# Words of w1 fetched a pair ahead, a product bank taken from attention's pool, and batch 1's attention one border sooner

## The chip, the cores and the metric

The kernel runs on one core of one Trainium2 chip. The metric is the device time of one execution in microseconds (us). One profiled execution is shown as a trace; all rows quoted here are from it. The engines are called PE (matrix multiplications; PEld is its loading of weights), DVE (vector engine), ACT (scalar engine), POOL (GpSimd) and SP (which here only issues transfers). SBUF is the on-chip memory, PSUM the eight banks that PE writes its sums into.

## The reference

Two layers follow each other. The first is attention in chunks of 32 tokens, each with a context of 16 tokens to its left and 8 to its right and 8 memory tokens (4 batches, 8 heads, 768 tokens, 64 channels a head). The second mixes tokens with a product of rank 32 and channels with a two-layer network:

```python
scores = scale * np.matmul(q_c, k_full.transpose(0, 1, 3, 2))
a = np.exp(scores - max); a = a / (sum(a) + 1e-9)
out[:, :, c_start:c_end] = np.matmul(a, v_full)
...
h = x.transpose(0, 2, 1) @ U @ V
u = x + h.transpose(0, 2, 1)
ch = np.maximum(u @ w_ch1, 0.0) @ w_ch2          # 512 -> 2048 -> 512
return u + ch
```

U, V and both weights arrive as 64-bit floats. The kernel decodes them on the chip into a float32 value, which it splits into a high and a low half for PE.

## The kernel before, in words

Each of the 4 batches has 768 tokens, in two blocks of 384. Hidden channels come in 16 groups f of 128.

**Batch 0** (`both_blocks`) goes through 32 units n. Units 0 to 17 take groups 0 to 8 of both blocks in turn, 18 to 24 groups 9 to 15 of block 0, 25 to 31 groups 9 to 15 of block 1. A unit is a w1_step (12 matmuls of 384 columns, L1178) and then a w2_step (9 matmuls of 512 columns, L1231 and L1236), which belongs to the unit before it. Unit 24 does two w2_steps, so unit 25 has none. Meanwhile the weights are decoded: ACT and DVE use the V buffers `vbs` (vb_104, vb_105, vbe) as working space, and the decoded values of each w1 group are kept in DRAM (`val_d`, vald in the rows).

**Batches 1 to 3** (`fast`, `seven`) replace the first layer of the network, for the two blocks and a pair p of groups at once, by seven products instead of eight (a Strassen scheme). Pairs p run from 0 to 7. `products(p)` does seven products of 6 matmuls each, in three PSUM banks b1, b2, b3, in the order b1, b2, b3, b1, b2, b3, b1. After each, ACT or DVE reads the bank: L1448 and L1454 (ACT, b1), L1450 and L1457 (DVE, b2), L1452 and L1459 (DVE, b3), L1461 (DVE, b1 after the last). The banks are drawn from two pools: ps_h (2 banks) and ps_a (3 banks, shared with attention and its turnings). Which bank of a pool one gets is the one that comes free first.

The seven weight factors of pair p+1 are made ahead, during products(p): `prepare` fetches the values of both groups (POOL's queue, L1335) into two rotating slots called val and lets POOL form five sums (L1341); `build_factor` casts a sum, or a half of the fetched words, on ACT (L1410) and takes the rest on DVE (L1411). ACT, DVE and POOL each work their instructions off in the order written, and POOL issues its transfers in that same order.

After products(p), `first_block` runs the second layer for block 0 (two w2_steps), except after products(0) and products(4), where the next products follow at once. After pair 3 and after pair 7 `second_block` runs block 1's second layer, its three accumulators being two ps_h banks and one ps_a bank.

**Attention of batch b+1** is woven into batch b at borders. It is a generator whose steps are, for each pair of heads s = 0 to 3: scores(s) (L713, then the softmax on DVE and ACT), the turning of its weights (L745, six transposes), and the weighing of V (L756). Then come the gathering of the token product (L864, L1057), two groups of three matmuls that add it to x (L1081, with the additions L1083), and the fold (L1363 to L1378), which turns x into the operands th and tl of the products. In batch 0 the list PLAN says at which of 26 borders (two in each of the units 19 to 31, one before the w1_step and one after it) a step is taken. From unit 29 on, `following` runs what is left of the attention and one third of the fold after the border.

The third in order is SP's queue: it issues the loads of q, k and v for the attention (L508, L527, L531) in the order in which the generator asks for them, between stores and loads of the low halves of w1 (L356, L437).

Of the kernel before, what the change touches and what calls it, by code (L numbers as in the profile page):

```python
# [9 lines left out]
F32 = mybir.dt.float32  # L10
# [36 lines left out]
RATEL = 6  # L47
RATES = 8
RATEB = 5
PLAN = [0, 1, 0, 0, 0, 1, 1, 1, 0, 1, 1, 1, 0, 1, 1, 1, 0, 1, 1, 1, 1, 1, 0, 0, 0, 0]  # L50
SUMS = ((0, 0, 0, 0, 1, "add"), (2, 0, 0, 1, 1, "add"), (4, 1, 0, 1, 1, "add"),
        (5, 0, 1, 1, 1, "subtract"), (6, 1, 0, 0, 0, "subtract"))
PRODUCTS = ((6, 0), (2, 1), (0, 2), (1, 0), (5, 1), (4, 2), (3, 0))
# [4 lines left out]
def chunk_attn_then_mixer_kernel(  # L58
# [13 lines left out]
    nc = tc.nc  # L72
# [1172 lines left out]
    def both_blocks(following):  # L1245

        units = []
        for f in range(SPLIT + LEAD):
            if f < SPLIT:
                units.append((0, f, 0, f == 0, None))  # L1250
            if f >= LEAD:
                g = f - LEAD
                units.append((1, g, 1, g == 0, False if g == SPLIT - 1 else None))
        units += [(0, f, 0, False, True if f == NF - 1 else None) for f in range(SPLIT, NF)]
        units += [(1, f, 0, f == SPLIT, True if f == NF - 1 else None) for f in range(SPLIT, NF)]
        prev = []
        for n, (blk, f, where, begins, ends) in enumerate(units):
            while done[0] < min(2 * NF, 2 * f + 1 + (n > LATE)):
                advance(1)
                more_w()  # L1260
            if n == 2:
                head.close()
            let_go()
            solo = n >= 2 * SPLIT
            if n == 2 * SPLIT:
                paced.close()
            for blk_, m, *_ in units[n:n + AHEAD + 1]:
                if m >= SPLIT and blk_ == 1:
                    get_w1l(m)
            w1l = w1ls[f]  # L1270
            if f >= SPLIT or blk == 1:
                del w1ls[f]
            if n == 2 * SPLIT - SOON or 2 * SPLIT - LAID <= n < 2 * SPLIT - LAID + 2:
                place(1)
            serve(RATEL if n < 2 * SPLIT else RATES)
            if n > 2 * SPLIT:
                border()
            if n == 0:
                for c, g3 in rest[:2]:
                    join_uT1(turn_x1(c), c, g3)  # L1280
            if n == len(units) - 1:
                for m in range(3):
                    build_factor(0, m)
            hid_ = w1_step(0, blk, f, w1l)
            if n == len(units) - 2:
                prepare(0)
            if n == len(units) - 5:
                open_turned()
            if n == len(units) - 1:
                open_fast()  # L1290
                for m in range(3, len(PRODUCTS)):
                    build_factor(0, m)
            if n == 0:
                decode(2, 4)
                for c, g3 in rest[2:]:
                    join_uT1(turn_x1(c), c, g3)
                decode(1, 1)
                decode(2, 6)
                decode(1, 6)
                decode(3, 2)  # L1300
            for _ in range(RATE + (3 < n < 12)):
                advance(1)
                more_w()
            if n > 2 * SPLIT:
                border()
            if n >= len(units) - 3:
                following()
            prev.append((blk, f, where, begins, ends) + hid_)
            if solo or n % 2 == 0 or ends:
                while len(prev) > (not ends):  # L1310
                    while done[0] < 2 * prev[0][1] + 2:
                        advance(1)
                        more_w()
                    w2_step(0, *prev.pop(0))
# [12 lines left out]
    def border():  # L1327
        place(PLAN[at[0]])
        at[0] += 1

    def prepare(p):

        whole = [slot([P, NCK, P], F32, "val") for _ in range(2)]
        for side in range(2):
            nc.gpsimd.dma_start(out=whole[side], in_=val_d[2 * p + side])  # L1335
        mixed[p, 1], mixed[p, 3] = whole[1][:, 2:4, :], whole[0][:, 0:2, :]
        for m, (n, fa, ca, fb, cb, op) in enumerate(SUMS):
            if m % 2 == 0:
                two = slot([P, 2, 2, P], F32, "sums")
            a, b_ = (whole[f][:, 2 * c:2 * c + 2, :] for f, c in ((fa, ca), (fb, cb)))  # L1340
            nc.gpsimd.tensor_tensor(out=two[:, m % 2], in0=a, in1=b_, op=getattr(ALU, op))  # L1341
            mixed[p, n] = two[:, m % 2]
# [80 lines left out]
    def seven(b, kept, last):  # L1423

        th, tl = turned[0]
        ta, tb = fast_pools[1]
        made = {}

        def products(p):
            banks = [ps_h.tile([P, 512], F32, name="ps_h"), ps_a.tile([P, 512], F32, name="ps_a")]  # L1430
            banks.append(ps_h.tile([P, 512], F32, name="ps_h"))
            banks = [bank_[:, :TOK] for bank_ in banks]
            b1, b2, b3 = banks
            kept[2 * p], kept[2 * p + 1] = (
                fast_pools[0].tile([P, TOK], F32, name="kept", bufs=NF // 2) for _ in range(2)
            )
            hid_ = {}
            for n, (i, at_) in enumerate(PRODUCTS):
                s = factors.pop((p, n))
                parts = [(s, c, t, c) for c in range(2) for t in (th, tl)] + [(s, 2 + c, th, c) for c in range(2)]  # L1440
                for m, (w, wc, t, c) in enumerate(parts):
                    nc.tensor.matmul(  # L1442
                        out=banks[at_], lhsT=w[:, wc, :], rhs=t[:, i, c, :], start=(n < 3 and m == 0),
                        stop=(m + 1 == len(parts)), skip_group_check=True,
                    )
                with tc.high_priority(offset=HIGH):
                    if n == 0:
                        nc.scalar.copy(out=ta, in_=b1)  # L1448
                    elif n == 1:
                        nc.vector.tensor_tensor(out=ta, in0=b2, in1=ta, op=ALU.subtract)  # L1450
                    elif n == 2:
                        nc.vector.tensor_tensor(out=tb, in0=b3, in1=ta, op=ALU.add)  # L1452
                    elif n == 3:
                        nc.scalar.copy(out=kept[2 * p], in_=b1)  # L1454
                    elif n == 4:
                        hid_[1] = split_hidden(b2)
                        nc.vector.tensor_tensor(out=tb, in0=tb, in1=b2, op=ALU.subtract)  # L1457
                    elif n == 5:
                        nc.vector.tensor_tensor(out=ta, in0=b3, in1=ta, op=ALU.add)  # L1459
                    else:  # L1460
                        nc.vector.tensor_tensor(out=kept[2 * p + 1], in0=b1, in1=tb, op=ALU.add)  # L1461
                        hid_[0] = split_hidden(ta)
                    if p + 1 < NF // 2 or not last:
                        for m in ((), (), (0,), (1, 2), (), (3, 4), (5, 6))[n]:
                            build_factor((p + 1) % (NF // 2), m)
                if n in (2, 6):
                    fast_border()
            made[p] = hid_

        def first_block(p):  # L1470
            hid_ = made.pop(p)
            for side in (1, 0):
                f = 2 * p + side
                ends = True if p == NF // 2 - 1 and side == 0 else None
                w2_step(b, 0, f, 0, p == 0 and side == 1, ends, *hid_[side])
                fast_border()

        def second_block(fs, ends, each):
            for f in fs:
                hid_ = split_hidden(kept.pop(f))  # L1480
                w2_step(b, 1, f, 2, f == fs[0], ends if f == fs[-1] else None, *hid_)
                each()

        return products, first_block, second_block

    def fast(b, following):
        n = NF // 2
        products, first_block, second_block = seven(b, {}, b == B - 1)
        passed[0] = 0
        for p in range(n):  # L1490
            if p + 1 < n or b + 1 < B:
                prepare((p + 1) % n)
            products(p)
            if p % (n // 2):
                first_block(p - 1)
            if p == n // 2 - 1:
                first_block(p)
                recall(b, 1)
                second_block(list(range(n)), False, fast_border)
        recall(b, 0)  # L1500
        first_block(n - 1)
        recall(b, 1)
        second_block(list(range(n, NF)), True, following)
# [73 lines left out]
```

## Time and profile before

| | |
|---|---|
| median of 3 runs | 653.23 us (651.63 to 653.72) |
| the profiled execution's own time | 654.93 us |
| its span, first to last instruction | 653.2 us |
| PE busy | 619.0 us (95%) |
| DVE, ACT, POOL busy | 458.8, 293.4, 189.9 us |
| mean granted clock of PE | 0.987 of full speed |

PE is busy in 95% of the span, so the time is its work plus its idle stretches. Most of the idle stands in the first 60 us, which the change does not touch. The rest is some twenty waits of 0.2 to 2.1 us. Two stretches of 20 us later on show a granted clock of 0.91. The rows below show each wait with what ended it; a busy share over the whole span would not.

### The profile page before, as it was taken

How to read it: one execution, taken by the hardware profiler on the slowest of the kernel's cores; microseconds unless marked ns; L12 is line 12 of the kernel's file. 1: busy time of each engine (PE TensorE's matmuls, PEld its weight loads, DVE VectorE, ACT ScalarE, POOL GpSimd, SP SyncE). 2: the span in 40 equal slices, each digit the busy share in tenths (PEclk: the TensorE clock that was granted, in tenths of full speed). 3: DMA queues.
4: the chain of work that ended last, by engine and by line, in shares of the span. 5: the costliest groups of instructions: out<-in, count | busy, mean ns of one | idle time of the engine just before them, and what ended most of it. 6: DMA issues, size and time to landing. Idle time of an engine off the chain costs nothing.

```text
span 653.2 us, 15318 instructions
## 1 busy us (share of the span) xinstructions
PE 619.0 (95%) x6052; PEld 537.6 (82%) x6054; DVE 458.8 (70%) x983; ACT 293.4 (45%) x700; POOL 189.9 (29%) x294
## 2 busy tenths in 40 slices
PE   7687999999899999999999999999999999999997
PEld 6556999987786798878898898988798799889986
DVE  4875998889555988756676969766776966427542
ACT  4656776655223545533334545532333643314321
POOL 3520011000002764004631663003731564006400
PEclk9889999999898999999999999999999999999999
DMA  9996679655996239976211439942221442003411
GB/s 204 170 287 253 223 213 247 160 148 140 155 206 126 80 131 167 150 107 130 97 50 65 153 122 153 165 57 82 72 75 43 143 154 82 2 16 97 129 48 50
DMA packets 157082, 84.17 MB, mean 129 GB/s; under 512 B 128978, under 2 KB 143314, under 8 KB 157010
## 3 DMA queue, kind: packets, MB, share of 16 engines
q1 hardware_dynamic: 146034, 47.40, 36.2%
q0 software_dynamic: 10976, 35.79, 16.4%
q8 instruction: 48, 0.79, 0.5%
q14 instruction: 24, 0.20, 0.1%
HBM read 63.63 MB, written 19.40 MB: 127 GB/s over the span
## 4 chain that ended last, share of the span: by engine, by line
PE 59%; issue 18%; DVE 11%; DMA 6%; ACT 2%; POOL 2%; SPq 1%; POOLq 0%; DVEq 0%; ACTq 0%
PE ps_h L1442 17%; PE acc L1231 10%; PE ps_a L1442 7%; PE ps_h L1231 5%; PE acc L1236 5%; PE ps_h L1236 2%; PE ps_a L1231 2%; DVE tl L1378 2%; DMA vb<-in_v_dram 2%; DVE fold L1373 1%; PE ps_a L756 1%; PE ps_a L713 1%; PE ps_a L1236 1%; DMA val<-vald 1%; POOL vald L374 1%
## 5 line engine op out<-in xcount | busy, mean ns | idle before, releaser
L1341 POOL TENSOR_TENSOR sums<-val 128x256 f32<-128x256 f32 x120 | 98.0, 847 | 56.9 <-DMA val<-vald 43.9
L1231 PE MATMUL acc<-w,hh 128*128 128x512 f32 x366 | 98.0, 403 | 1.0 <-DVE w L382 1.0
L1442 PE MATMUL ps_h<-th,w1l 128*128 128x384 f32 x288 | 84.2, 344 | 6.5 <-DVE part L1459 5.0
L1231 PEld LDWEIGHTS acc<-w,hh 128*128 128x128 f32 x366 | 67.9, 190 | 16.2 <-issue 1.8
L1442 PEld LDWEIGHTS ps_h<-th,w1l 128*128 128x128 f32 x288 | 53.0, 188 | 12.1 <-ACT pT L747 3.6
L1418 DVE SCALAR_TENSOR_TENSOR hl<-kept,hh 128x384 fp32r<-128x384 f32 x48 | 28.8, 599 | 40.3 <-PE ps_a L1236 23.0
L1442 PE MATMUL ps_h<-th,s 128*128 128x384 f32 x192 | 52.8, 336 | 0.0
L1236 PE MATMUL acc<-w,hl 128*128 128x512 f32 x183 | 51.9, 392 | 0.0
L1442 PE MATMUL ps_h<-tl,w1l 128*128 128x384 f32 x144 | 49.0, 340 | 0.9 <-DVE tl L1378 0.9
L1417 ACT ACTIVATE hh<-kept 128x384 fp32r<-128x384 f32 x48 | 25.2, 526 | 54.0 <-PE ps_a L1231 29.2
L1231 PE MATMUL ps_h<-w,hh 128*128 128x512 f32 x156 | 43.4, 400 | 0.0
L1178 PE MATMUL ps_h<-uh,w1h 128*128 128x384 f32 x124 | 42.5, 349 | 0.8 <-ACT uh L1150 0.8
L1178 PE MATMUL ps_h<-ul,w1h 128*128 128x384 f32 x124 | 41.2, 340 | 0.0
L1236 PEld LDWEIGHTS acc<-w,hl 128*128 128x128 f32 x183 | 34.4, 189 | 7.8 <-issue 0.2
L1448 ACT COPY part<-ps_h 128x384 f32<-128x384 f32 x24 | 11.5, 480 | 62.8 <-PE ps_h L1442 54.6
L1231 PE MATMUL ps_a<-w,hh 128*128 128x512 f32 x132 | 37.9, 390 | 1.8 <-ACT hh L1184 1.8
L1163 POOL DMA_DIRECT2D xd<-x x9 | 4.9, 543 | 114.5 <-DVE x L1192 113.7
L1410 ACT CAST s<-sums 128x256 fp32r<-128x256 f32 x72 | 28.6, 402 | 17.1 <-PE ps_h L1442 13.7
L1411 DVE TENSOR_TENSOR w1l<-sums,w1l 128x256 fp32r<-128x256 f32 x48 | 25.4, 529 | 14.8 <-ACT w1l L1410 14.8
L1442 PEld LDWEIGHTS ps_h<-th,s 128*128 128x128 f32 x192 | 35.0, 188 | 0.0
L1231 PEld LDWEIGHTS ps_h<-w,hh 128*128 128x128 f32 x156 | 28.2, 188 | 5.7
L1184 ACT ACTIVATE hh<-ps_h 128x384 fp32r<-128x384 f32 x31 | 15.0, 487 | 38.7 <-PE ps_h L1178 38.7
(290 smaller groups left out, 1469.4 us busy)
## 6 DMA issues: line engine op xcount, KB each, us to landing
val<-vald POOLq DMA_DIRECT2D x48, 256.0 KB, 3.1
vb<-in_v_dram SPq DMA_DIRECT2D x23, 336.0 KB
rw<-in_moe_w_ch_dram SPq DMA_DIRECT2D x14, 512.0 KB
x<-xd POOLq DMA_DIRECT2D x27, 256.0 KB, 4.0
raw<-in_moe_w_ch_dram SPq DMA_DIRECT2D x20, 256.0 KB
kall<-in_k_dram SPq DMA_DIRECT2D x48, 96.0 KB
kall<-in_q_dram SPq DMA_DIRECT2D x48, 96.0 KB
out_dram<-x POOLq DMA_DIRECT2D x18, 256.0 KB, 3.0
```

The source lines that it names most:

```text
L1178: nc.tensor.matmul(out=ph[:, :TOK], lhsT=w[:, c, :], rhs=u[c], start=(m == 0), stop=(m + 1 == len(parts)),)
L1184: nc.scalar.activation(out=hh, in_=ph[:, :TOK], func=AF.Relu)
L1231: nc.tensor.matmul(out=acc[tt], lhsT=h[:, sl], rhs=w, start=(begins and m == 0), stop=False,)
L1236: nc.tensor.matmul(out=acc[tt], lhsT=hl[:, sl], rhs=w2h[f], start=False, stop=ends is not None)
L1341: nc.gpsimd.tensor_tensor(out=two[:, m % 2], in0=a, in1=b_, op=getattr(ALU, op))
L1378: nc.vector.tensor_tensor(out=tl[:, i:i + m, :, sl], in0=f32[n][:, 0:m], in1=th[:, i:i + m, :, sl].bitcast(F32), op=ALU.subtract,)
L1410: nc.scalar.copy(out=s[:, 0:2], in_=total)
L1411: nc.vector.tensor_tensor(out=s[:, 2:4], in0=total, in1=s[:, 0:2].bitcast(F32), op=ALU.subtract)
L1417: nc.scalar.activation(out=hh, in_=src, func=AF.Relu)
L1418: vpace[0] = nc.vector.scalar_tensor_tensor(out=hl, in0=src, scalar=0.0, in1=hh.bitcast(F32), op0=ALU.max, op1=ALU.subtract,)
L1442: nc.tensor.matmul(out=banks[at_], lhsT=w[:, wc, :], rhs=t[:, i, c, :], start=(n < 3 and m == 0), stop=(m + 1 == len(parts)), skip_group_c ...
L1448: nc.scalar.copy(out=ta, in_=b1)
```

## The change

Four edits go together.

1. The words of pair p no longer go into rotating slots. They have one fixed place, the last 512 columns of vb_104 and vb_105, which no V of batches 1 to 3 uses. `fetch_words` is taken out of `prepare` and called a pair sooner: for pair p+2 behind products(p).
2. The first sums (`prepare(0)`) move from unit 30 to unit 26; the words of pair 1 are fetched behind unit 31's factors.
3. In products(0) and products(4), b1 is a ps_a bank and b2 a ps_h bank.
4. PLAN loses one of the three zeros in front of its third placement and has one more placement at its end: every step from the first turning on comes one border sooner, and the first three of the additions of the token product come at a border of their own.

```diff
-PLAN = [0, 1, 0, 0, 0, 1, 1, 1, 0, 1, 1, 1, 0, 1, 1, 1, 0, 1, 1, 1, 1, 1, 0, 0, 0, 0]
+PLAN = [0, 1, 0, 0, 1, 1, 1, 0, 1, 1, 1, 0, 1, 1, 1, 0, 1, 1, 1, 1, 1, 1, 0, 0, 0, 0]
...
-            if n == len(units) - 2:
+            if n == len(units) - 6:
+                fetch_words(0)
                 prepare(0)
...
                 for m in range(3, len(PRODUCTS)):
                     build_factor(0, m)
+                fetch_words(1)
...
-    def prepare(p):
+    whole = [
+        vb.rearrange("p i d -> p (i d)")[:, NX * D:NX * D + CH].rearrange("p (c f) -> p c f", c=NCK) for vb in vbs[:2]
+    ]
-        whole = [slot([P, NCK, P], F32, "val") for _ in range(2)]
+    def fetch_words(p):
         for side in range(2):
             nc.gpsimd.dma_start(out=whole[side], in_=val_d[2 * p + side])
+
+    def prepare(p):
+
         mixed[p, 1], mixed[p, 3] = whole[1][:, 2:4, :], whole[0][:, 0:2, :]
...
             banks = [ps_h.tile([P, 512], F32, name="ps_h"), ps_a.tile([P, 512], F32, name="ps_a")]
+            if p % (NF // 4) == 0:
+                banks.reverse()
             banks.append(ps_h.tile([P, 512], F32, name="ps_h"))
...
             products(p)
+            if p + 2 < n or b + 1 < B:
+                fetch_words((p + 2) % n)
```

On PE, in units 21 and 22 of batch 0, the first turning (L745) and the steps behind it move against the w1_step (L1178) and the w2_step (L1231, L1236); L756 is the weighing of heads pair 0, L713 the scores of heads pair 1.

```order
 L1236 MATMUL acc_1273<-w_1788,hl 128x512
 L1236 MATMUL acc_1274<-w_1788,hl 128x512
+L745 MATMUL ps_a<-ident,pt 128x128 x6
 L1178 MATMUL ps_h<-uh,w1h_1912 128x384
 L1178 MATMUL ps_h<-ul,w1h_1912 128x384
...
 L1178 MATMUL ps_h<-uh,w1l 128x384 x4
-L745 MATMUL ps_a<-ident,pt 128x128 x6
+L756 MATMUL ps_a<-vb_104,pT 32x64 x48
 L1231 MATMUL acc_1272<-w_1883,hh 128x512 x2
 L1231 MATMUL acc_1273<-w_1883,hh 128x512 x2
```

The turning now stands ahead of unit 21's w1_step, and the weighing has the turning's old place behind it.

On SP, at the same place, the loads of V for heads pair 1 (L527, L531) stand against two stores and a load of low halves (L356, L437).

```order
 L356 DMA w1ld_126<-w1l 128x512
 L508 DMA kall<-in_k_dram 32x24x32 x4
-L356 DMA w1ld_127<-w1l 128x512
-L356 DMA w1ld_128<-w1l 128x512
-L437 DMA w1l<-w1ld_123 128x512
 L527 DMA vb_104<-in_mem_v_dram 8x24x64
 L531 DMA vb_104<-in_v_dram 56x24x64
 L527 DMA vb_104<-in_mem_v_dram 8x24x64
 L531 DMA vb_104<-in_v_dram 56x24x64
+L356 DMA w1ld_127<-w1l 128x512
+L356 DMA w1ld_128<-w1l 128x512
+L437 DMA w1l<-w1ld_123 128x512
```

The V loads follow the k loads directly, and the three transfers of w1 come behind them.

On POOL, at pair 4 of batch 1, the recall of three x tiles (L1168) and three stores (L1163) stand ahead of the sums of pair 5. Before:

```order
L1168 DMA x<-xd_5_151 128x512
L1163 DMA xd_3_149<-x 128x512
L1163 DMA xd_4_150<-x 128x512
L1163 DMA xd_5_151<-x 128x512
L1335 DMA val<-vald_140 128x512
L1335 DMA val<-vald_141 128x512
L1341 TENSOR_TENSOR sums<-val 128x256 x5
```

And now:

```order
L1339 DMA vb_104<-vald_140 128x512
L1339 DMA vb_105<-vald_141 128x512
L1168 DMA x<-xd_3_149 128x512
L1168 DMA x<-xd_4_150 128x512
L1168 DMA x<-xd_5_151 128x512
L1163 DMA xd_3_149<-x 128x512
L1163 DMA xd_4_150<-x 128x512
L1163 DMA xd_5_151<-x 128x512
L1348 TENSOR_TENSOR sums<-vb_104 128x256
L1348 TENSOR_TENSOR sums<-vb_104,vb_105 128x256
```

The fetch of the words (L1339) has moved ahead of the recall and the stores; the sums (L1348) follow the stores with no fetch between.

## Rows read from the trace of the kernel before

**Rows 1.** Waits of PE, whole span: engine, line, releaser: total us, times, longest.

```profile
PE ps_h L1442 <- DVE part L1459: 5.0, 5, 1.7
PE ps_a L756 <- DMA vb<-in_v_dram: 4.2, 3, 2.1
...
PE ps_h L1442 <- DVE x L1192: 1.0, 2, 0.5
...
PE ps_h L1442 <- DVE tl L1378: 0.9, 2, 0.5
...
PE ps_a L1442 <- DVE tl L1378: 0.7, 1, 0.7
```

**Rows 2.** Timeline of PE, batch 1, pair 5: start us, us, instruction [idle before].

```profile
310.34 0.41 PE L1442 MATMUL ps_h<-th,w1l 128*128 128x384 f32 x1 [1.72 <-DVE part L1459]
310.59 0.34 PE L1442 MATMUL ps_h<-tl,w1l 128*128 128x384 f32 x1
310.77 0.34 PE L1442 MATMUL ps_h<-th,w1l 128*128 128x384 f32 x1
```

**Rows 3.** Timelines of POOL and DVE, batch 1, pair 4.

```profile
305.57 3.87 POOL L1341 TENSOR_TENSOR sums<-val 128x256 f32<-128x256 f32 x5 [3.39 <-DMA val<-vald]
...
308.56 0.54 DVE L1457 TENSOR_TENSOR part<-part,ps_a 128x384 f32<-128x384 f32 x1
...
309.65 0.54 DVE L1459 TENSOR_TENSOR part<-ps_h,part 128x384 f32<-128x384 f32 x1
```

**Rows 4.** Timelines of PE and ACT, batch 0, the first turning.

```profile
146.93 0.96 PE L745 MATMUL ps_a<-ident,pt 128*128 128x128 f32 x6 [1.04 <-ACT pt L734]
...
146.35 0.94 ACT L734 ACTIVATE pt<-pt 128x384 f32<-128x384 f32 x2
```

**Rows 5.** Timelines of PE and DVE, the scores of heads pair 1.

```profile
154.98 1.16 PE L713 MATMUL ps_a<-kall 64*32 64x64 f32 x94 [0.92 <-DVE xa L765]
...
154.38 1.01 DVE L765 TENSOR_TENSOR xa<-ps_a,rs 128x384 f32<-128x384 f32 x2
```

**Rows 6.** Timelines of SP and PE, the load of V for heads pair 1 and its weighing.

```profile
152.25 2.33 SPq L508 DMA_DIRECT2D kall<-in_k_dram  x4
...
161.22 0.48 SPq L531 DMA_DIRECT2D vb<-in_v_dram  x1
...
166.45 1.59 PE L756 MATMUL ps_a<-vb,pT 64*32 64x64 f32 x94 [2.13 <-DMA vb<-in_v_dram]
```

**Rows 7.** Two stretches: busy us of each engine (instructions), granted clock, DMA share, GB/s.

```profile
160.00:180.00 20.00, 16.69 (x260) 14.13 (x259) 12.34 (x31) 6.41 (x16) 1.62 (x3) 0.91 1.00 158
...
200.00:220.00 20.00, 18.93 (x92) 15.49 (x91) 16.33 (x31) 9.27 (x22) 8.77 (x13) 0.91 0.45 107
```

**Rows 8.** Timelines of PE and DVE, the weighing of heads pair 2 and what follows.

```profile
181.22 1.15 PE L756 MATMUL ps_a<-vb,pT 64*32 64x64 f32 x94 [1.30 <-DMA vb<-in_v_dram]
...
179.23 0.56 DVE L1185 SCALAR_TENSOR_TENSOR hl<-ps_h,hh 128x384 fp32r<-128x384 f32 x1 [0.99 <-ACT hh L1184]
...
180.60 0.94 DVE L703 STREAM_TRANSPOSE kall<-kall 128x768 f32<-128x768 f32 x1
```

**Rows 9.** Timeline of PE, the additions and the first fold.

```profile
203.29 0.87 PE L1081 MATMUL ps_a<-g,v 96*128 96x512 f32 x3
...
206.73 1.71 PE L1363 MATMUL ps_a<-ident,xa 128*128 128x128 f32 x8
```

**Rows 10.** Timelines of DVE, POOL and PE, the fold and batch 1's first products.

```profile
210.22 3.31 DVE L1378 TENSOR_TENSOR tl<-fold,th 128x512 fp32r<-128x512 f32 x4
...
217.75 2.21 DVE L1378 TENSOR_TENSOR tl<-fold,th 128x512 fp32r<-128x512 f32 x4
...
211.08 4.80 POOL L1341 TENSOR_TENSOR sums<-val 128x256 f32<-128x256 f32 x5 [2.12 <-DMA val<-vald]
...
228.22 0.44 PE L1442 MATMUL ps_h<-tl,w1l 128*128 128x384 f32 x1 [0.47 <-DVE tl L1378]
```

**Rows 11.** Timeline of POOL, batch 1, pair 0: the sums of pair 2.

```profile
233.76 4.20 POOL L1341 TENSOR_TENSOR sums<-val 128x256 f32<-128x256 f32 x5 [3.08 <-DMA val<-vald]
```

## The prediction

> **What bounds the kernel now.** I read the list of PE's waits first, then the timeline around each, then the two stretches with a lower clock. PE is busy in 95% of the span, so nothing but idle on PE, or its clock, can be won. In the list, four sums belong to places that the change touches: 5.0 us in five waits for L1459, 1.0 in two for the additions L1192, 4.2 in three for V and 1.6 (0.9 and 0.7) in three for tl [rows 1]. The reader is to see that these are small sums of a few waits each, so the change is worth single microseconds a place. In the timelines the reader is to look at who was late: for L1459 it is the sums on POOL, two engines back [rows 3].
>
> What a wait costs beyond its idle: matmuls last 0.34 us but start 0.18 apart (310.59, 310.77), and the first after a wait is followed after 0.25 [rows 2]. The pipe has to fill again, 0.16 and 0.07 us; I count 0.25 a wait.
>
> **Part A: banks and words in batches 1 to 3.** The first bank of products(1) and products(5) is the ps_h bank that comes free first, b3 of the products before, read by L1459. In the pair 4 case, the five sums began at 305.57 after a wait of 3.39 for the words, the factors followed on ACT and DVE, and L1459 ran at 309.65, while PE could have gone on 1.72 us before 310.34 [rows 2, 3]. Two things now change. With b1 on ps_a, the ps_h bank that comes free first is b2's, read by L1457, which stood 1.1 us ahead of L1459 (308.56) even when late [rows 3] and is due two products, 12 x 0.18 = 2.1 us, before the next pair. And the words are there when POOL comes to the sums, so the 3.39 go. All five waits go: 5.0. The two for L1192 go too, since the ps_a bank needs no addition of block 1 in ps_h and the ps_h banks are asked for 6 x 0.18 = 1.1 us later: 1.0. Seven restarts: 1.75. Sum: +7.8, bounds 5 (some L1459 waits turn into waits for ps_a) and 7.8; I take the upper end, since at the border behind pair 4 the two banks of the scores have long been read.
>
> What A costs: the words have one place, so the fetch for pair p+2 waits for the factor of pair p+1 that is cast straight from the words (the sixth of seven products). POOL stands there; behind it only sums and recalls wait, none needed within 4 us. Between products(0) and (1), and (4) and (5), there is no first_block, so pair 2's sums may come later than now, where they began at 233.76, as products(1) did, after 3.08 of landing [rows 11]. Late factors stand in front of bank reads on ACT and DVE. Nothing shows this directly: 0 if the factors just keep up, 0.6 at each of six places if the last product waits. I take 0.2 each, nearer to rows 11: -1.2.
>
> **Part B: batch 0's end.** Step by step.
>
> The first turning: it could start at 146.93 because ACT's exponential began only at 146.35; PE had already idled 1.04 behind unit 21's w1_step [rows 4]. Now this w1_step (12 x 0.18 = 2.1) comes behind the turning, and nothing makes the exponential earlier, so the wait grows to about 3.1. The scores of heads pair 1 are held by DVE's L765 at 154.38 in both orders [rows 5], so I have PE there at 155.0 as before, but with one w1_step less done: -2.1 (bounds 0 and -3.6, the latter if the clock falls as below and nothing hides it).
>
> The weighing of heads pair 1: V's second half was issued at 161.22, behind k (152.25), two stores and a load, and PE stood until 166.45 [rows 6]. In the new order it follows k at once, and k can start sooner, since the transposition of keys that frees its place stands four DVE instructions earlier. V is then issued when the first weighing ends, near 152, and lands 5.2 later (166.45 less 161.22), near 158; PE comes to it near 163. The waits 2.13 and 0.8 (4.2 in all less 2.13 and 1.30) go [rows 1, 6, 8], with a restart: +3.2. After that wait the granted clock fell: 0.91 over 20 us is 1.8 us of clock [rows 7]; with no wait it stays up: +1.5, since part of the stretch PE was idle. Bounds 0 and 5.
>
> The weighing of heads pair 2 waited 1.30 for V [rows 8]; that goes, +1.6 with a restart. But unit 25 has no w2_step, so the scores of heads pair 3 follow the weighing directly. They need DVE's L1185 (0.56), L703 (0.94) and one half of L765 (1.01 for two), after 0.5 for ACT: 2.5 from the end of the w1_step, of which the weighing covers 1.15 [rows 5, 8]. New wait 1.4 and a restart: -1.7. Net -0.1, bounds -2 and +1.6.
>
> The additions: six matmuls and the first fold took 206.73 - 203.29 = 3.4 for 1.3 of work, as each of the second three waits for a bank [rows 9]. Now a w1_step lies between the two groups; the fold still waits for one addition. I take 0.9 lost instead of 2.1: +1.2. Behind it the clock fell again, 0.91 [rows 7]: +1.5, bounds 0 and 1.8.
>
> The entry of batch 1: the three waits for tl, of which the last ended at 228.22, had 1.6 idle, with restarts 2.4 [rows 1, 10]. DVE is full from the additions on, and PE now comes earlier as well. What shortens DVE's path: the first sums are formed near 180, not beside the fold. With POOL in sums, four tl took 3.31, without 2.21 [rows 10]: 1.1 saved, and two factors and three additions leave the path. I leave a wait of 1.0: +1.4, bounds 0 and 2.4.
>
> The Trainium skill (SBUF — State Buffer, section Who interferes with whom) says that a DVE instruction with two SBUF inputs and a GpSimd instruction that reads SBUF exclude each other, the second to issue being blocked until the first is done. The trace agrees that they slow each other, with 3.31 against 2.21, but not by a whole sum (0.96) each [rows 10]. By the page, four tl beside pair 1's sums would cost 2.7 us more at batch 1's entry, and the result would be 642.7.
>
> Sum of B: -2.1 + 4.7 - 0.1 + 2.7 + 1.4 = +6.6. In all 7.8 - 1.2 + 6.6 = 13.2. The profiled execution took 654.93 (653.2 span and 1.7 around it): 641.7. It lies 1.7 above the median 653.23, so I forecast **640.0** on that scale.
>
> **The rivals.**
> 1. V stays late. SP's transfers were near their limit in this stretch (DMA share 1.00) [rows 7], so V may land with the wait, and the longer first wait brings the clock down a second time. For it: that share. Against it: k starts four DVE instructions sooner, in a stretch in which nothing else loads. B loses 4.7 and another 1.5: 640.0 + 6.2 = 646.
> 2. The words do not help: held by the one place, sums come as late as now, and only the bank change works. Then the two pair 4 waits that sums caused leave half of their 3.2, and the first sums save nothing at the entry: 640.0 + 1.6 + 1.4 + 1 = 644.
> 3. Slower. The one place turns the fetch into a chain: factor, fetch, landing, sums, factor. With a landing of 3.1 to 3.4 [rows 3, 11] and a sum of 0.84 (4.20 for five), pair 2's first factor is ready some 4 us after products(1) start, 0.8 after it is due (18 x 0.18 = 3.2); the last product, 36 x 0.18 = 6.5 after the start, waits only if the landing takes some 5. Each us beyond that is one us at each of six places: at 8 it costs 18 against a gain of 14.4: 657. Against it: no row shows such a landing here.
> 4. The gains of B are given back, by new clock falls at the first turning and at unit 25 and by DVE at the entry, and A's waits become waits for ps_a: 651 to 653.
>
> **How the numbers follow.** Forecast 0.64, rival 1 0.14, rival 2 0.10, rival 3 0.06, rival 4 0.06. Range: downward, the first turning hidden (2.1), no late factors (1.2), the entry free (1.0), the additions free (0.9): about 634.5. Upward it takes in rivals 1 and 2 with a margin for the clock: 649. So 634 to 649. What lies within 0.3% (2 us) cannot be told from no change here. Faster by more than that: 0.64 + 0.14 + 0.10 = 0.88; the same 0.06; slower 0.06.
>
> **What would show it.** Right: no wait for L1459 at pairs 1 and 5, sums of pair 5 starting right behind the stores, a wait of about 3 us at the first turning, none for V, one of 1 to 2 us at the scores of heads pair 3, clock 1.00 around the fold. Wrong: waits for V that remain; ps_a waits at products(4); ACT or DVE waiting for sums in products(1) and (5) with PE behind them; the third bank of batch 1's first products less than 5 us earlier than 228.22.

## The result, and the profile after

The changed kernel takes 643.34 us (median of 6 runs, 639.25 to 647.77) against 653.48 beside it: a ratio of 0.9837, 95% interval 0.9801 to 0.9873. It ran in two more series, with medians of 647.02 (ratio 0.9895) and 643.97 (0.9832); over all 18 runs the median is 644.3. Over all runs that is 9 to 10 us less, in the second series alone 6.5, where 13.2 were forecast. Both kernels scatter: the 63 runs of before beside all series of this document lie between 648.7 and 660.9 us, the 18 of the changed kernel between 639.3 and 650.3.

The profiled execution is the longest of the first six (647.77, span 644.9: 2.9 us lie outside the span, in the next two 1.8). I therefore read two more executions of the same kernel, of 640.96 and 644.35, and say which is which: first, second, third.

PE's waits over the whole span, first execution (line, releaser: total us, times, longest), without those of the first 60 us, which the change does not touch:

```profile
PE ps_a L745 <- ACT pt L734: 3.6, 1, 3.6
...
PE acc L1236 <- issue: 2.0, 1, 2.0
PE ps_a L1231 <- ACT hh L1184: 1.8, 1, 1.8
...
PE ps_a L713 <- DVE kall L703: 1.0, 1, 1.0
...
PE ps_a L713 <- DVE xa L765: 0.7, 1, 0.7
...
PE ps_a L756 <- ACT pT L747: 0.7, 1, 0.7
...
PE ps_h L1451 <- DVE tl L1385: 0.7, 2, 0.5
...
PE ps_h L1451 <- DVE part L1461: 0.5, 2, 0.2
PE ps_h L1451 <- ACT part L1457: 0.5, 2, 0.3
```

Of [rows 1] the waits for L1459 (now L1468), for L1192 and for V are gone; tl has 0.7 left of 1.6. The first turning waits 3.6, the weighing behind it has a new wait of 0.7 for ACT's copy of the turned weights (pT), and a wait of 2.0 has no releaser (the list says "issue": the profile shows nothing that PE waited for). The 1.8 for L1184 stands in before as well, near 65 us.

**Where the time went, place by place.** I take the start of the same row of PE in both kernels and subtract. Between the first turning and the scores of heads pair 3 the new order has one w1_step less done; there I add its 2.1. The change from one mark to the next, in us, minus for sooner:

```
up to                                   forecast    first   second   third
the first scores (same work)                   0     -1.5     -2.6    -1.1
the first turning                        } +2.1     +2.5     +2.5    +2.2
end of the scores of heads pair 1        }          +2.0     +0.7    +1.7
end of the scores of heads pair 2           -4.7     -3.4     -3.4    -3.4
end of the scores of heads pair 3           +0.1     -0.7     -0.7    -0.7
the first fold                              -1.2     +2.2     -1.5    +0.1
the first products of batch 1               -1.5     -1.5     -1.5    -1.5
the last matmuls                            -8.0     -8.0     -7.7    -7.9
sum                                        -13.2     -8.3    -14.1   -10.6
```

The first line is no effect of the change: the profiled execution of before was late there (136.15; in the ten other profiles with the same order up to there it lies between 133.6 and 135.6). Without it the three give -6.8, -11.6 and -9.5. Five of the lines below it agree to 0.4 us in all three executions; two vary, the end of the scores of heads pair 1 and the first fold. The next section is on these.

### The profile page after: what moved, and what is told of

It reads as the page before. It is cut to its first block, busy times and chain, and to the rows that moved or that the text cites. A ratio compares the mean times of both kernels' runs of the same rounds, so it can differ in the third digit from the quotient of the medians.

```text
span 644.9 us, 15304 instructions
## 1 busy us (share of the span) xinstructions
PE 615.7 (95%) x6052; PEld 537.4 (83%) x6054; DVE 450.9 (70%) x983; ACT 293.9 (46%) x700; POOL 186.6 (29%) x294
## 4 chain that ended last, share of the span: by engine, by line
PE 71%; issue 10%; DVE 7%; DMA 6%; ACT 2%; POOL 2%; SPq 2%; DVEq 0%; POOLq 0%; ACTq 0%
PE ps_h L1451 17%; PE acc L1231 11%; PE ps_a L1451 8%; PE ps_h L1231 6%; PE acc L1236 6%; PE ps_h L1178 3%; PE ps_a L1231 3%; PE ps_h L1236 3%; PE ps_a L713 2%; PE ps_a L756 2%; PE ps_a L1236 1%; PE ps_h L1223 1%; PE ps_a L745 1%; PE ps_a L1370 1%; DMA rw<-in_moe_w_ch_dram 1%
## 5 line engine op out<-in xcount | busy, mean ns | idle before, releaser
L1231 PE MATMUL acc<-w,hh 128*128 128x512 f32 x366 | 96.9, 399 | 1.0 <-DVE w L382 1.0
L1231 PEld LDWEIGHTS acc<-w,hh 128*128 128x128 f32 x366 | 67.3, 188 | 15.7 <-issue 1.5
L1451 PE MATMUL ps_h<-th,w1l 128*128 128x384 f32 x264 | 76.5, 343 | 0.6 <-ACT part L1457 0.5
L1348 POOL TENSOR_TENSOR sums<-vb,vb 128x256 f32<-128x256 f32 x72 | 58.4, 823 | 4.2 <-DMA vb<-vald 2.8
L1348 POOL TENSOR_TENSOR sums<-vb 128x256 f32<-128x256 f32 x48 | 38.3, 798 | 61.3 <-DMA vb<-vald 43.6
L1236 PE MATMUL acc<-w,hl 128*128 128x512 f32 x183 | 52.1, 392 | 2.0 <-issue 2.0
L1418 DVE TENSOR_TENSOR w1l<-sums,w1l 128x256 fp32r<-128x256 f32 x48 | 28.4, 592 | 34.5 <-ACT w1l L1417 34.5
L1451 PEld LDWEIGHTS ps_h<-th,w1l 128*128 128x128 f32 x264 | 48.6, 188 | 3.9 <-issue 1.7
L1339 POOL DMA_DIRECT2D vb<-vald x48 | 26.3, 550 | 82.8 <-issue 39.3
L1451 PE MATMUL ps_h<-tl,w1l 128*128 128x384 f32 x132 | 44.9, 340 | 0.7 <-DVE tl L1385 0.7
L1231 PE MATMUL ps_h<-w,hh 128*128 128x512 f32 x156 | 43.2, 399 | 0.0
L1178 PE MATMUL ps_h<-uh,w1h 128*128 128x384 f32 x124 | 43.2, 355 | 0.0
L1236 PEld LDWEIGHTS acc<-w,hl 128*128 128x128 f32 x183 | 34.4, 188 | 10.0 <-issue 2.5
L1178 PE MATMUL ps_h<-ul,w1h 128*128 128x384 f32 x124 | 42.1, 348 | 0.0
L1231 PE MATMUL ps_a<-w,hh 128*128 128x512 f32 x132 | 37.9, 391 | 1.8 <-ACT hh L1184 1.8
L1451 PE MATMUL ps_a<-th,w1l 128*128 128x384 f32 x120 | 36.0, 340 | 0.0
L1231 PEld LDWEIGHTS ps_h<-w,hh 128*128 128x128 f32 x156 | 28.2, 188 | 5.7
```

The source lines that it names most:

```text
L1178: nc.tensor.matmul(out=ph[:, :TOK], lhsT=w[:, c, :], rhs=u[c], start=(m == 0), stop=(m + 1 == len(parts)),)
L1231: nc.tensor.matmul(out=acc[tt], lhsT=h[:, sl], rhs=w, start=(begins and m == 0), stop=False,)
L1236: nc.tensor.matmul(out=acc[tt], lhsT=hl[:, sl], rhs=w2h[f], start=False, stop=ends is not None)
L1418: nc.vector.tensor_tensor(out=s[:, 2:4], in0=total, in1=s[:, 0:2].bitcast(F32), op=ALU.subtract)
L1451: nc.tensor.matmul(out=banks[at_], lhsT=w[:, wc, :], rhs=t[:, i, c, :], start=(n < 3 and m == 0), stop=(m + 1 == len(parts)), skip_group_c ...
```

## The first turning, V, and a wait without a releaser

Timelines of PE, DVE and ACT at the first turning, first execution:

```profile
141.73 0.43 DVE L236 TENSOR_SCALAR vb<-vb 128x512 int32<-128x512 int32 x1 [2.25 <-DMA vald<-vb]
142.07 1.01 DVE L725 TENSOR_REDUCE mx<-ps_a 128x6 f32<-128x384 f32 x2
...
145.29 0.93 ACT L734 ACTIVATE pt<-pt 128x384 f32<-128x384 f32 x2
...
145.86 1.54 PE L745 MATMUL ps_a<-ident,pt 128*128 128x128 f32 x6 [3.56 <-ACT pt L734]
...
147.52 0.52 PE L1178 MATMUL ps_h<-ul,w1h 128*128 128x384 f32 x1
147.84 0.52 PE L1178 MATMUL ps_h<-uh,w1h 128*128 128x384 f32 x1
...
152.71 0.72 PE L756 MATMUL ps_a<-vb,pT 64*32 64x64 f32 x48 [0.69 <-ACT pT L747]
...
151.28 0.49 ACT L1184 ACTIVATE hh<-ps_h 128x384 fp32r<-128x384 f32 x1 [2.16 <-PE ps_h L1178]
...
152.17 0.48 ACT L747 COPY pT<-ps_a 128x384 f32<-128x384 f32 x1
```

Two stretches of all engines around it and around the wait without a releaser (busy us and instructions of PE, PEld, DVE, ACT, POOL; granted clock, DMA share, GB/s), first execution:

```profile
145.00:150.00 5.00, 4.14 (x15) 4.14 (x16) 5.00 (x11) 4.12 (x11) 0.00 (x0) 0.50 0.32 52
...
190.00:195.00 5.00, 5.00 (x113) 4.65 (x112) 0.75 (x2) 1.45 (x3) 2.11 (x4) 0.75 0.07 19
```

The corresponding stretches of the second execution, which is earlier by then (the wait at the turning is there too, 3.59; the other is not):

```profile
145.00:150.00 5.00, 4.92 (x66) 4.22 (x64) 4.89 (x9) 3.83 (x11) 0.00 (x0) 0.66 0.49 79
185.00:190.00 5.00, 5.00 (x118) 4.43 (x117) 1.58 (x3) 1.35 (x3) 2.81 (x4) 1.00 0.60 163
```

The reader is to see the order on DVE: the maxima L725 of the first scores stand behind a decoding step, L236, that waits 2.25 us for the store of its buffer. The exponential comes at 145.29, PE waits 3.56, and then the clock stands at 0.50, its lower level of 1.2 GHz: matmuls of w1_step start 0.32 apart (147.52, 147.84) instead of 0.18. From the start of the turning to the start of the scores of heads pair 1, which is the same work in both kernels, the three executions take 1.9 to 2.9 us longer than before. Of this, 0.69 is the new wait for pT: the w1_step now stands between the turning and the weighing, and ACT takes its L1184 before the second copy. The rest is the clock. Before's wait of 0.92 at the scores [rows 5] is gone in return, so the row of the table shows 0.7 to 2.0.

The weighing of heads pair 1 and what comes behind it, timelines of SP and PE, first execution:

```profile
153.77 0.34 SPq L531 DMA_DIRECT2D vb<-in_v_dram  x1
...
164.19 1.17 PE L756 MATMUL ps_a<-vb,pT 64*32 64x64 f32 x96
...
168.68 1.15 PE L713 MATMUL ps_a<-kall 64*32 64x64 f32 x94 [0.72 <-DVE xa L765]
...
181.13 1.55 PE L713 MATMUL ps_a<-kall 64*32 64x64 f32 x96 [1.00 <-DVE kall L703]
...
188.83 0.61 PE L1236 MATMUL acc<-w,hl 128*128 128x512 f32 x1 [2.03 <-issue]
```

V is issued at 153.8 instead of 161.2 [rows 6] and no weighing waits for it. The scores behind it wait for DVE: 0.72 at heads pair 2, 1.00 at heads pair 3.

The wait at 188.83 names no engine. While it lasted, the DMA queues carried this (queue, kind: packets, MB, share of 16 engines; 186.1 to 188.9 us):

```profile
q1 hardware_dynamic: 536, 0.56, 68.9%
q0 software_dynamic: 16, 0.03, 4.6%
q8 instruction: 1, 0.02, 2.3%
q14 instruction: 1, 0.01, 1.8%
```

The one packet of queue q8, 16 KB of instructions, lasted from 186.17 to 187.22, while the data queues took 73% of the engines. The Trainium skill (Runtime: NRT & Kernel Launch, section Instruction fetch mechanics) says that an engine's sequencer fetches its next block of 256 instructions by a DMA queue of its own, mostly hidden. The trace fits a block that came late: PE and its weight loads have 12106 instructions, some 47 times 256, and q8 carries 47 or 48 such packets in an execution. Over all 14 profiles PE has 30 waits of more than 0.3 us without a releaser, and each ends 1.1 to 1.9 us after the last packet of q8 has landed (1.6 here). But no run takes the fetch away or moves it, so the cause is not shown by an experiment. What the runs show is also how often PE stood so near 186 us: for 0.7 to 2.0 us in the profiles of 8 of the 11 executions with the new PLAN or the early words, the first of them fetched at unit 26 (here 2.03, none, 1.47), each time among the three matmuls L1236 of one w2_step, and in none of the three with neither.

**The products.** Timelines of POOL, ACT and PE, batch 1, pairs 4 to 6, first execution:

```profile
296.65 1.90 POOL L1163 DMA_DIRECT2D xd<-x  x3 [29.04 <-DVE x L1192]
298.57 0.75 POOL L1348 TENSOR_TENSOR sums<-vb 128x256 f32<-128x256 f32 x1
...
305.44 1.11 POOL L1339 DMA_DIRECT2D vb<-vald  x2 [3.34 <-DVE rs L737]
308.48 0.73 POOL L1348 TENSOR_TENSOR sums<-vb 128x256 f32<-128x256 f32 x1 [1.93 <-DMA vb<-vald]
...
309.24 0.41 ACT L1417 CAST w1l<-sums 128x256 fp32r<-128x256 f32 x1 [1.48 <-POOL sums L1348]
...
310.07 0.44 PE L1451 MATMUL ps_h<-th,w1l 128*128 128x384 f32 x1 [0.16 <-ACT part L1457]
```

The sums of pair 5 begin at 298.57, right behind the stores, not 3.39 after them [rows 3]. Those of pair 6 show the price of the one place: fetched at 305.44, they wait 1.93, ACT's first factor 1.48, PE 0.16. Four waits of 0.16 to 0.31 inside the products of pairs 4 and 5, in batches 1 and 2, are what is left in batches 1 to 3, behind the two for tl at the entry.

## The experiments

All totals are medians of fresh runs; the medians of before beside them are 653.5 to 655.5. "Batches 1 to 3" is from the first matmul of batch 1's products to the last row of PE in the profiled execution: 425.4 in before, 417.4, 417.7 and 417.5 in the changed kernel.

**x1_again, x11_third_time** (no edit).

> The changed kernel once more, unchanged. In its first profiled execution (647.8 us against a median of 643.3) PE stood 2.0 us at 188.8 with no releaser, and the clock fell behind it. Theory A (that stand belongs to the one execution): no such wait near the scores of heads pair 3 in this profile, the fold then starts at about 204 and the span is 640 to 642; median 643. Theory B (the stand is part of the new order): the wait of about 2 us is there again, span near 645, and the median of 643 has another source.

> The changed kernel a third time, beside the run with the first scores one border sooner. Its two series so far had medians of 643.3 and 647.0 with 639 to 650 in each. Theory A (single executions differ by stands of PE without a releaser near 186 us and the clock behind them, so the series differ by chance): about 644.5 here, and the profile has such a stand or a total near 641. Theory B (the second series was the odd one): 643 or less, like the kernel with the scores sooner.

Measured 647.02 (640.96 to 650.31) and 643.97 (641.09 to 644.90). The profile of x1 has no wait near 186 and a total of 640.96, that of x11 one of 1.47 and 644.35. So theory A of x1 holds for the profile, not for the median. Of x11 theory A came true, but 641 to 650 us within one series say that a single series of this kernel tells 1 or 2 us from nothing.

**x2_old_plan, x3_plan_alone.** The change without its new PLAN, and that PLAN alone:

```diff
-PLAN = [0, 1, 0, 0, 1, 1, 1, 0, 1, 1, 1, 0, 1, 1, 1, 0, 1, 1, 1, 1, 1, 1, 0, 0, 0, 0]
+PLAN = [0, 1, 0, 0, 0, 1, 1, 1, 0, 1, 1, 1, 0, 1, 1, 1, 0, 1, 1, 1, 1, 1, 0, 0, 0, 0]
```

> The changed kernel with the old table PLAN: banks, words and early sums alone. Theory A (part A carries the gain as forecast, some 6.6 us with the lighter entry of batch 1, and the sooner border adds 2 to 4): 645 to 647, against 653.5 before. Theory B (the sooner border is worth the forecast 5.2 us): 648 to 649. Theory C (the sooner border wins nothing, since the first turning and the clock take back what V gives): 642 to 644.

> The kernel before with the new table PLAN alone. Theory A: 650 to 652. Theory B (forecast): 648. Theory C: 653 to 655. In the profile all theories expect the longer wait at the first turning (3 us or more), no wait for V at the weighing of heads pair 1, and the five waits for L1459 as before.

Measured 647.92 (ratio 0.9924, 0.9888 to 0.9960), with batches 1 to 3 at 417.7, and 653.28 (0.9982, 0.9954 to 1.0011). The total of x2 lies just below theory B's range. PLAN alone gains nothing that can be measured (theory C). What it is worth on top of the banks and words is not settled: 3.6 us by x2's 647.9 and the 644.3 over all series, but 0.9 against the changed kernel run beside it (647.02); from the first scores to the first products x2's profile takes 88.1 us, the three of the changed kernel 88.7, 83.6 and 85.8. The profile of PLAN alone has batch 0 shorter by 2.3 (from the first scores to the first products 85.1, before 87.5), and batches 1 to 3 longer by 2.3: 427.65, with one wait of 2.1 for tl, 2.3 at pair 5 of batch 1, and a clock of 0.91 behind it (300 to 320 us): what came sooner waited longer for late sums. PE's waits, PLAN alone:

```profile
PE ps_h L1442 <- DVE part L1459: 5.6, 5, 2.3
PE ps_a L745 <- ACT pt L734: 3.6, 1, 3.6
...
PE ps_a L1442 <- DVE tl L1378: 2.1, 1, 2.1
...
PE acc L1236 <- issue: 1.3, 1, 1.3
```

**x5_banks_alone, x6_words_alone, x7_late_first_sums.** The kernel before with the reversal alone; with the words a pair ahead in their fixed place alone; and the change without the early first sums:

```diff
+            if p % (NF // 4) == 0:
+                banks.reverse()
```

```diff
-            if n == len(units) - 6:
+            if n == len(units) - 2:
                 fetch_words(0)
                 prepare(0)
```

> The kernel before with the reversal of the first two banks at pairs 0 and 4 alone. Theory A (the bank is what PE waited for; the ps_h banks are now asked for 1.1 and 2.1 us later than the late readers need): the five waits for L1459 and the two for L1192 all go even with the sums as late as before, 646 to 648. Theory B (late sums hold the products in any case): the pair 4 waits stay at half or more under another name, 649 to 651.

> The kernel before with the words of w1 fetched a pair ahead into their fixed place alone (first sums as late as before, banks and PLAN of before). Theory A (the bank): the waits for L1459 at pairs 1 stay at 0.4 to 0.8, those of pairs 5 fall from 1.7 and 1.5 to about 0.5, the two for L1192 stay: 650 to 652. Theory B (the words): all waits for L1459 go, 647 to 649. Rival of the prediction (the one place is a chain): above 655, with POOL, ACT or DVE late and PE behind them.

> The changed kernel with the first words fetched and the first sums formed at the second last unit again. Theory A (early sums lighten DVE's way into batch 1): the waits for tl at batch 1's entry grow from 0.7 to 2 or more, 646 to 648. Theory B (the early load of the words only crowds the transfers near 180 to 190 us, where PE then stands without a releaser): no such stand, runs closer together, 641 to 643.

Measured 651.48 (0.9943, 0.9916 to 0.9970), 648.39 (0.9907, 0.9883 to 0.9930) and 645.77 (0.9865, 0.9826 to 0.9903). Batches 1 to 3 take 422.5, 421.9 and 419.0: the banks give 2.8, the words 3.5, both 6.4, and the early sums the last 1.3 to 1.6. By these stretches, one profile each, the parts add up, but not wait by wait: the waits of 1.72 and 1.49 at pair 5 of batches 1 and 2 fall to 1.18 and 0.79 with the banks and go altogether with the words. The bank alone does not do (theory B of x5, the total 0.5 above its range): the waits for L1459 go, but at these two places PE waits for factors of sums that are as late as before. Timelines of POOL and PE, banks alone:

```profile
305.83 3.86 POOL L1341 TENSOR_TENSOR sums<-val 128x256 f32<-128x256 f32 x5 [3.95 <-DMA val<-vald]
...
309.50 0.41 PE L1444 MATMUL ps_h<-th,w1l 128*128 128x384 f32 x1 [1.18 <-ACT s L1410]
```

The words alone leave the bank's wait: 0.35 at each of the pairs 1 and 0.92 at pair 5 of batch 3. The two for L1192 are gone here too, so either edit removes them. The total is theory B's, the waits lie between both theories. The chain that rival 3 feared is not there. PE's waits and a stretch of all engines, words alone (L1466 is before's L1459):

```profile
PE ps_h L1449 <- DVE part L1466: 2.0, 4, 0.9
...
200.00:220.00 20.00, 18.92 (x99) 15.64 (x97) 18.78 (x40) 10.75 (x27) 9.25 (x13) 1.00 0.33 95
```

The stretch has a clock of 1.00, though x6 has the old PLAN and the waits of before at the additions (0.31 and 0.57; before 0.31 and 0.56). In x2 and x5, with the old PLAN as well, it is 0.91, as in before [rows 7]. So these waits alone do not decide whether the clock falls there.

With late first sums the two waits for tl are 0.79 and 1.16, 1.95 in all against 0.67 (theory A of x7), and a wait without releaser, 0.72, is there at 185.85 nonetheless, which speaks against the early words as its cause.

**x10_two_places.** Even pairs keep the fixed place, odd pairs get one of their own:

```diff
+        wholes[p] = fixed if p % 2 == 0 else [slot([P, NCK, P], F32, "val") for _ in range(2)]
```

> The changed kernel with a second place for the words (odd pairs in a place of their own). Theory A (the one place costs what was forecast, or the four waits of 0.2 to 0.3 us around pairs 4 and 5 of batches 1 and 2 come from it): batches 1 to 3, from the first product of batch 1 to the last matmul, take 415.5 to 416.7 in place of 417.4 to 417.7, and those waits go. Theory B (the one place costs nothing: the words are there in time): 417.4 to 417.8, the waits stay; the total differs only by batch 0.

Measured 645.65 (0.9865, 0.9826 to 0.9903); batches 1 to 3 take 420.6. Neither theory: of the four small waits the two in pairs 5 go, the two in pairs 4 stay, three of 0.43 to 0.52 come in pairs 1, and the waits for tl are 1.66 in all. A second place made this way does not pay; why pairs 1 suffer stays open.

**x4_scores_sooner, x12_scores_sooner_again, x9_border_ahead, x8_v_first.** Four attempts on the first turning: the first scores one border sooner; the same again; the border written ahead of the unit's decoding; and x4 with the attention's loads ahead of those of w1's low parts.

```diff
-PLAN = [0, 1, 0, 0, 1, 1, 1, 0,
+PLAN = [1, 0, 0, 0, 1, 1, 1, 0,
```

```diff
+            if n > 2 * SPLIT:
+                border()
             for _ in range(RATE + (3 < n < 12)):
                 advance(1)
                 more_w()
-            if n > 2 * SPLIT:
-                border()
```

```diff
+            if n > 2 * SPLIT:
+                serve(RATES)
             for blk_, m, *_ in units[n:n + AHEAD + 1]:
                 if m >= SPLIT and blk_ == 1:
                     get_w1l(m)
...
-            serve(RATEL if n < 2 * SPLIT else RATES)
+            if n <= 2 * SPLIT:
+                serve(RATEL if n < 2 * SPLIT else RATES)
```

> The changed kernel with the first scores one border sooner too (PLAN begins 1, 0 in place of 0, 1). Theory A (the first turning waits because the exponential of ACT stands behind decoding on DVE and ACT, and moves up with the scores): the wait of 3.6 us at the first turning falls to 1 to 2.5 and the clock stays up there, 639 to 642. Theory B (the exponential stays where it is, since the decoding ahead of it waits for a store of a buffer): the wait stays at 3.3 or more and the time at 643 to 644.

> The changed kernel with PLAN beginning 1, 0, a second time. Theory A (the wait at the first turning and the clock behind it are gone for good, 3 to 4 us): 640 to 642, 3 us or more below the changed kernel run beside it. Theory B (the lead of the first series was chance): within 1.5 us of the changed kernel.

> The changed kernel, with the second border of each of batch 0's units 19 to 31 written ahead of the decoding of that unit instead of behind it, so that the softmax of the first scores stands ahead of the decoding on DVE and ACT while PE's order stays. Theory A (the first turning waits on DVE's and ACT's order alone): its wait of 3.6 us falls below 1 without the 1.65 us that scores one border sooner waited for the additions to x; the clock stays up there; 639 to 641. Theory B (the decoding that is pushed back is missed elsewhere: the closing of block 0 waits for w2last): a wait for w2last or w1 of 1 to 3 us in its place, 642 to 645.

> The run with scores one border sooner, and in each unit of the attention's part the attention's loads issued ahead of those of w1's low parts. Theory A (V for heads pair 2 is late because of its place behind two 256 KB loads): its wait of 1.95 us falls below 0.7 and the clock stays up behind it, 638 to 640. Theory B (the transfers are at their limit, order does not matter): the wait stays above 1.3, 641 us as without it, or another load is late in its place.

Measured: x4 640.93 (0.9807, 0.9769 to 0.9846) beside 647.02 of x1; x12 642.77 (0.9821) beside 643.97 of x11; x9 642.65 (0.9820, 0.9772 to 0.9868); x8 641.64 (0.9799, 0.9770 to 0.9828). The turning with the scores sooner, x4, PE and ACT:

```profile
133.69 0.30 PE L713 MATMUL ps_a<-kall 64*32 64x64 f32 x2 [1.35 <-DVE x L1192]
...
142.59 0.94 ACT L734 ACTIVATE pt<-pt 128x384 f32<-128x384 f32 x2 [0.59 <-DVE pt L730]
...
144.42 0.82 PE L745 MATMUL ps_a<-ident,pt 128*128 128x128 f32 x6
...
176.57 1.24 PE L756 MATMUL ps_a<-vb,pT 64*32 64x64 f32 x94 [1.95 <-DMA vb<-in_v_dram]
```

The exponential moves from 145.29 to 142.59 and the turning waits no more: what bound it was the order on DVE and ACT. In its place PE waits 1.65 for the additions to x at the scores (1.35 and 0.30) and 1.95 for V of heads pair 2, which it now reaches too soon, with a clock of 0.50 behind that wait (178 to 184 us). x9 keeps PE's order and wins a part: the maxima move up, but DVE still meets the store of a buffer ahead of the differences that the exponential needs, and the wait is 2.19, with a clock of 0.50 behind it (146 to 148 us); w2last is not waited for. So neither theory of x9 holds: the total lies in B's range, without B's wait. Timelines of DVE, ACT and PE, x9:

```profile
141.64 0.43 DVE L236 TENSOR_SCALAR vb<-vb 128x512 int32<-128x512 int32 x1 [0.85 <-DMA vald<-vb]
...
143.93 0.93 ACT L734 ACTIVATE pt<-pt 128x384 f32<-128x384 f32 x2
...
144.50 0.97 PE L745 MATMUL ps_a<-ident,pt 128*128 128x128 f32 x6 [2.19 <-ACT pt L734]
```

In x8 the wait for V is gone and a part of w1 is late in its place (1.59 at 183.67): theory A for the wait, theory B for the time. x4 and x12 together (12 runs) have a median of 642.2, x8 641.6, against 644.3 of the changed kernel: 2 us that single series hardly separate. In the last pair of series it is 1.2 where theory A expected 3: by the total theory B of x12 came true, though the wait at the turning and the clock fall behind it are gone.

## Why the prediction was right, and where it was too high

- **What bounds**: right. Every wait that went is one that the list of PE's waits named, and beside the waits only the clock paid.
- **Banks and words, with the entry of batch 1** (7.8 - 1.2 + 1.4 = 8.0): 7.7 to 8.0 in three executions. All seven waits went; the two for L1192, put down to the bank, go with the words alone as well (x6). The cost of the one place was taken as 1.2; the two small waits that go with a second place are 0.16 and 0.31, with a restart each 1.0. The four small waits that are left cost 0.94 and 1.0 of restarts (first execution), more than the 1.2, and the entry has 0.67 of wait left, less than the 1.0: that the sum comes so close is in part luck. By the estimate that the prediction made from the rule on shared reads in the Trainium skill (SBUF — State Buffer, section Who interferes with whom), a whole sum for each tl, the entry would have been 2.7 worse. In the first execution the two tl beside POOL's sums took 0.78 and 0.71 us, against 0.68 for one with no sum beside it (227.49 in before): 0.03 to 0.10 more, not a whole sum. A block for the rest of a sum, as the rule has it, is not excluded by that.
- **The first turning** (-2.1): the step that failed. The wait came as forecast (3.56, about 3.1 expected), but "I have PE there at 155.0 as before" did not hold. Measured from the first scores, PE came to the main part of these scores (154.98 in before) 2.1, 1.1 and 1.8 us later than before: the clock fell behind the wait, and the weighing waits 0.69 for pT, for which no term stood. With the w1_step the loss is 3.2 to 4.5. I had the fall only as the lower bound of -3.6 and in rivals 1 and 4.
- **V** (+4.7): 3.4. V was in time as worked out, and the clock stood at 1.00 (160 to 180 us) as forecast. Missing was a new wait at the scores of heads pair 2, 0.72 and a restart: without V's delay DVE's L765 is the late one there too.
- **Heads pair 2 and 3** (-0.1): +0.7; the new wait is 1.00, not 1.4.
- **The additions** (+1.2) and **the clock at the fold** (+1.5): 1.5 and 1.5 where nothing disturbs. Of the 2.1 that the additions lost before, the trace lists 0.87 as waits, in two of the second three matmuls. That the clock falls there because of them is not shown: in x6 it does not. In two of the three executions the wait without a releaser (in one with the clock behind it) took 3.7 and 1.6 of the first. No row of before shows that wait, and no term stood for it.
- **The rivals**: a second fall of the clock at the first turning, half of rival 1, came true; V was in time. Rivals 2 and 3 fall with x6. Of rival 4 the same fall came true, the waits for ps_a and the loss at the entry did not.
- **The signs**: all that were named for right came, and two named for wrong. In products(5) ACT waits 1.48 for sums with PE 0.16 behind it; that is small, as priced. And the third bank of batch 1's first products was to be 5 us earlier than 228.22 at least, and is 1.5, 7.5 and 3.9 earlier, which counts the same loss in batch 0.
- **The range**: its lower end adds up to 634.8, not 634.5, and the last 1 us in rival 2's sum has no row; neither bears on the outcome.

In the third execution, the nearest to the median, the 3.7 us too much are 1.8 at the first turning (the clock and the wait for pT), 1.3 at V (the new wait) and 1.3 ahead of the fold (the wait without a releaser), less 0.8 at heads pair 3. I counted two falls of the clock that end and not the one that the longer first wait begins.

## What to carry to other kernels

Where a clock fall is booked as a gain because a wait goes, look for the wait that the same change makes longer: a first wait grown from 1 to over 3 us brought the fall with it in each of the three executions, and one of 2.19 in x9. A buffer that is asked for in another order and data that comes a step sooner each gave their part, 2.8 and 3.5 us, and together 6.4, though some waits shrank by either; run them apart to know. A step taken sooner moved PE here only to the next thing that was late (PLAN alone: 653.28 against 653.52 beside it).

## What had not been expected of the hardware

PE stood 0.7 to 2.0 us with no releaser in the list, near 186 us, in 8 of the 11 profiles with the new PLAN or the early words; in x12 it stood so for 1.57 at 274.6 as well. Each of these stands ended 1.4 to 1.7 us after a packet of instructions had landed in queue q8. In one of the two executions of the changed kernel that had it the clock fell behind it (0.75 from 190 to 195 us in the first), in the other it did not (1.00, third). It accounts for a part of the difference between the three profiles. The executions of before lie as far apart, and their one profile has no such stand, so the scatter as a whole stays open.
